# One pool of eight PSUM banks, and more work for the DMA transposes, in a fused attention and channel-mix kernel

## The chip, the cores and the metric

The kernel runs on one core of a Trainium2 chip. The metric is the device time of one execution in microseconds, as the median of several runs. A profile is one execution recorded instruction by instruction; its span, from the first to the last instruction, is a little shorter than its device time.

## What is computed

Sliding-window attention with a linear position bias (batch 8, 8 heads, 576 positions, head size 64, window 128) feeds a channel mix of width 512 with an inner width of 1024. Inputs and output are float32; the kernel computes in bfloat16 and accumulates in float32.

```python
scores = scale * q @ k.T                      # per batch and head, 576 x 576
mask   = (rel >= 0) & (rel < 128)             # rel = query position - key position
scores = where(mask, scores - slope[h] * |rel|, -1e9)
x      = softmax(scores) @ v                  # heads side by side: (8, 576, 512)

x_prev = x shifted by one position
xk = mu_k * x + (1 - mu_k) * x_prev
xr = mu_r * x + (1 - mu_r) * x_prev
k  = relu(xk @ w_k)                           # 512 -> 1024
out = sigmoid(xr @ w_r) * (k * k @ w_v)       # 1024 -> 512
```

## The kernel before

**Attention.** A batch has four head pairs g. For each, q and k are brought into a transposed layout `qk` or `qx` (64 head elements of two heads on 128 partitions). `scores` (its matmuls are L726, in batch 0 with a bias product, L713) multiplies keys by queries with 64 rows, both heads at once on the two halves of the array, only inside the window; the keys' 4.5 blocks of 128 are done in two halves, HALF0 and HALF1, each with up to 512 columns for each of two heads, which is two banks of PSUM. ScalarE takes the exponential (L740) into `at`, VectorE multiplies by a mask (L753) that holds window and bias, and `attend` (L781) multiplies by v with a column of ones, so that the denominators come out beside the sums; VectorE takes reciprocals (L787) and writes the normalized `xu` (L793).

**Transposes.** The output `xu` has positions on the partitions, the channel mix wants channels there (`xt`). Three ways are in use, chosen by batch: `out_t` by full transposes on TensorE (L820, batch 0), `out_some` by half transposes on TensorE in two row tiles for two head pairs at a time (L837, batches in `OH`) with a ScalarE copy out of PSUM (L696), and `out_flip` by a DMA transpose on SP's queue (batches in `XO`; the crossbar). The same holds for q and k: TensorE (`qk_quad`, `qk_some`: L1078, L837) up to batch 3, DMA transposes (`flip`, `qx<-cb`) from batch 4 on. The last 64 positions of q and k, the tails, go through `tails_full` (four transposes on TensorE, L912, and a VectorE copy) or through `tail_flip` (a DMA transpose `tt<-ts`, batches in `XTT`). A change between matmuls that use 64 rows of the array and those that use 128 is called a row change here.

**Channel mix.** `shift` forms x minus its predecessor (`dl`, L880) and the two mixtures `xk`, `xr` (L887) on VectorE. `channel_mix` then runs over pieces of 256 to 512 positions: eight groups of four matmuls with `wk_sb` (L983), a relu on ScalarE (L990), a square on VectorE or ScalarE (L964, L962); per 128 positions four matmuls with `wr_sb` (L1001), a tanh on ScalarE (L1008), eight with `wv_sb` (L1017) and VectorE's product of both (L1022), which SP's queue stores (L1047).

**Order.** Every step is a node of a plan. `ORDER` gives TensorE, ScalarE and VectorE a fixed sequence of nodes, written out in the file; the plan walks through it with assumed durations and hands out buffers (`Hold`, by class) as they come free, and in doing so sets the order of SP's and POOL's queues. Engines then wait for each other by semaphores. 90 small matmuls on a zero tile (`warm`, L687) are nodes like others and stand where the order puts them. Loads are issued by POOL with a cast to bfloat16.

**PSUM.** Two tiles of two banks (`duo`, class `p2`) serve scores and attention; four of one bank (`uno`, class `p1`) serve all the rest. Both halves of a head pair's scores are one node, which takes both `duo` at once:

```python
_, (m0, m1) = scores(b, g, [HALF0 + (None,), HALF1 + (htt,)], ...)
```

`n_split` halves some of the late stores, so that the number of hardware DMAs is a multiple of eight.

## Time and profile before

| | |
|---|---|
| median of 3 runs | 229.41 us (228.8 to 229.55) |
| profiled execution | 228.84 us |
| its span | 227.1 us |
| TensorE (PE) busy | 221.8 us, 98% |
| VectorE (DVE) busy | 188.8 us, 83% |
| ScalarE (ACT) busy | 155.0 us, 68% |
| mean granted TensorE clock | 0.998 |

Lines of the profile name the engine (PE matmuls, PEld weight loads, DVE, ACT, POOL, SP), the source line, the operation, what it writes and reads, the count, the busy time, the mean duration in ns, and the idle time of the engine before it with what ended it. In a table by stage, each engine has its busy time and its count of instructions. The chain of waits runs from the last instruction back through whatever released each step; its rows show a start, a length and the work.

### The profile page before, as it was taken

The page shows a single profiled execution, that of the slowest core. Times are in us where ns is not written, and L with a number is a line of the kernel's source. Part 1 is how long each engine was busy: PE and PEld are TensorE (multiplying, and loading weights), DVE is VectorE, ACT ScalarE, POOL GpSimd, SP SyncE. Part 2 cuts the span into 40 slices and gives each one's busy share as a digit, 9 for nine tenths or more (in the row PEclk, how much of TensorE's full clock was granted, in tenths as well). Part 3 has the DMA queues.
Part 4 walks back from the last instruction along what each step waited for, and adds up shares of the span by engine and source line. Part 5 has one row for each costly group of instructions (what it writes and reads, how often), then busy time and mean ns, then how long its engine had stood idle before and what let it go on. Part 6 is the DMA issues. An engine that isn't in the chain of part 4 may idle for free.

```text
span 227.1 us, 6442 instructions
## 1 busy us (share of the span) xinstructions
PE 221.8 (98%) x2587; PEld 133.2 (59%) x2587; DVE 188.8 (83%) x423; ACT 155.0 (68%) x279; POOL 92.0 (41%) x118
## 2 busy tenths in 40 slices
PE   8899999999999999999999999999999999999994
PEld 8576766755666755556666554546765455446552
DVE  6786999899879998899978996999899988963433
ACT  0678999999989984975868358768567564047511
POOL 8856726599962964385208750240000000000000
PEclk9999999999999999999999999999999999999999
DMA  6999999999999999999999999999150415430124
GB/s 165 179 185 200 197 196 175 199 180 151 196 156 165 137 130 180 168 182 147 211 180 158 120 185 231 177 136 222 30 135 3 123 46 52 131 136 3 49 92 139
DMA packets 129981, 33.19 MB, mean 146 GB/s; under 512 B 116632, under 2 KB 126112, under 8 KB 129952
## 3 DMA queue, kind: packets, MB, share of 16 engines
q0 software_dynamic: 95728, 16.26, 97.5%
q1 hardware_dynamic: 32480, 15.94, 34.1%
q10 hardware_dynamic: 1744, 0.59, 1.1%
q8 instruction: 20, 0.33, 0.6%
q14 instruction: 9, 0.07, 0.1%
HBM read 33.56 MB, written 9.44 MB: 189 GB/s over the span
## 4 chain that ended last, share of the span: by engine, by line
PE 92%; ACT 3%; DMA 2%; SPq 1%; issue 0%; DVE 0%; DVEq 0%; ACTq 0%
PE uno L983 28%; PE uno L1017 28%; PE uno L1001 13%; PE duo L726 7%; PE duo L781 7%; DMA qx<-in_q_dram 2%; PE uno L837 2%; PE uno L1078 2%; ACT at L740 1%; PE duo L713 1%; ACT qk L696 1%; PE uno L781 1%; SPq L550 1%; PE uno L687 1%; PE uno L820 1%; PE uno L939 0%
## 5 line engine op out<-in xcount | busy, mean ns | idle before, releaser
L983 PE MATMUL uno<-xk,wk_sb 128*128 128x256 bf16 (+2 forms) x416 | 72.0, 314 | 0.1
L740 ACT ACTIVATE at<-duo 128x1024 bf16<-128x1024 f32 (+2 forms) x68 | 65.5, 985 | 8.8 <-PE duo L726 8.5
L1017 PE MATMUL uno<-wv_sb,kk 128*128 128x512 bf16 (+2 forms) x296 | 69.7, 374 | 0.0
L990 ACT ACTIVATE rl<-uno 128x256 bf16<-128x256 f32 (+2 forms) x104 | 46.4, 471 | 26.4 <-PE uno L983 21.0
L983 PEld LDWEIGHTS <-wk_sb 128*128 128x128 bf16 x416 | 38.7, 98 | 24.2 <-issue 0.3
L1017 PEld LDWEIGHTS <-kk 128*128 128x128 bf16 x296 | 27.2, 98 | 27.3
L500 POOL DMA_DIRECT2D vs<-in_v_dram x32 | 28.4, 904 | 31.8 <-PE duo L781 25.9
L753 DVE TENSOR_TENSOR at<-at,mask 128x1024 bf16<-128x1024 bf16 x56 | 36.9, 682 | 1.8 <-ACT at L740 1.8
L964 DVE TENSOR_TENSOR kk<-rl 128x256 bf16<-128x256 bf16 (+2 forms) x94 | 30.2, 339 | 8.8 <-ACT rl L990 8.4
L1008 ACT ACTIVATE rs<-uno 128x512 bf16<-128x512 f32 x36 | 21.1, 604 | 22.2 <-PE uno L1001 22.1
L1001 PE MATMUL uno<-wr_sb,xr 128*128 128x512 bf16 x144 | 36.1, 379 | 0.0
L1022 DVE SCALAR_TENSOR_TENSOR ot<-rs,uno 128x512 f32<-128x512 bf16 (+2 forms) x37 | 24.4, 666 | 10.5 <-PE uno L1017 8.8
L887 DVE SCALAR_TENSOR_TENSOR xk<-dl,mu_sb,xt 128x576 bf16<-128x576 bf16 (+1 forms) x32 | 24.4, 779 | 0.0
L887 DVE SCALAR_TENSOR_TENSOR xr<-dl,mu_sb,xt 128x576 bf16<-128x576 bf16 (+1 forms) x32 | 24.3, 776 | 0.0
L781 PEld LDWEIGHTS <-at 128*128 128x128 bf16 x576 | 21.0, 97 | 4.7 <-ACT at L740 0.4
L793 DVE TENSOR_TENSOR xu<-duo,rc 128x640 bf16<-128x640 f32 x28 | 22.6, 815 | 0.2
L1001 PEld LDWEIGHTS <-xr 128*128 128x128 bf16 x144 | 13.3, 98 | 13.5 <-issue 0.2
L531 POOL DMA_DIRECT2D cb<-in_k_dram x20 | 17.5, 888 | 6.9 <-DMA vs<-in_v_dram 4.7
L781 PE MATMUL duo<-vs,at 128*128 128x65 bf16 x448 | 18.6, 193 | 0.0
L531 POOL DMA_DIRECT2D cb<-in_q_dram x20 | 17.7, 935 | 1.2 <-PE duo L781 1.1
L696 ACT COPY xt<-uno 128x640 bf16<-128x640 bf16 (+3 forms) x28 | 15.0, 583 | 3.3 <-PE uno L837 2.5
L880 DVE TENSOR_TENSOR dl<-xt 128x576 bf16<-128x576 bf16 (+1 forms) x32 | 13.5, 432 | 2.8 <-ACT xt L696 2.7
(83 smaller groups left out, 197.9 us busy)
## 6 DMA issues: line engine op xcount, KB each, us to landing
out_dram<-ot SPq DMA_DIRECT2D x30, 256.0 KB, 4.6
vs<-in_v_dram POOLq DMA_DIRECT2D x32, 128.0 KB, 7.8
cb<-in_q_dram POOLq DMA_DIRECT2D x20, 128.0 KB, 6.3
cb<-in_k_dram POOLq DMA_DIRECT2D x20, 128.0 KB, 12.1
out_dram<-ot SPq DMA_DIRECT2D x10, 128.0 KB, 1.8
wk_sb<-in_moe_w_k_dram POOLq DMA_DIRECT2D x2, 512.0 KB, 9.1
cb<-in_q_dram POOLq DMA_DIRECT2D x4, 256.0 KB, 9.7
cb<-in_k_dram POOLq DMA_DIRECT2D x4, 256.0 KB, 8.6
```

The lines of the kernel that those rows point to most:

```text
L500: return dma(POOL, 256, issue_t(1024), lambda e: nc.gpsimd.dma_start(out=vs_buf[h.idx][:, j, :, 0:D], in_=v[b, :, 128 * j:128 * j + 128].r ...
L531: return [dma(POOL, 256, issue_t(1024), lambda e, r=r: nc.gpsimd.dma_start(out=cb_buf[h.idx][:, i, r], in_=src[:, :, r]), [g], kind="q") f ...
L740: lambda e, ah=ah, w=w, hp=hp: nc.scalar.activation(out=ah(), in_=two(hp)[:, :, 0:w], func=AF.Exp, scale=float(scale)), (), [hp])
L753: nc.vector.tensor_tensor(out=a, in0=a, in1=m, op=ALU.mult)
L781: nc.tensor.matmul(a[:, hl, t - t0], lhsT=at[:, lo:lo + 128], rhs=vs[:, u, 2 * g + hl, 0:W] if u < NF else tvb[:, 2 * g + hl, 0:W], start= ...
L887: lambda e: nc.vector.scalar_tensor_tensor(out=buf[hk.idx][:, g, e0 + c0:e0 + c1], in0=dls(), scalar=mu[:, g:g + 1], in1=xc(1), op0=ALU.mu ...
L964: nc.vector.tensor_tensor(out=out, in0=in_, in1=in_, op=ALU.mult)
L983: nc.tensor.matmul(one(hp)[:, 0:n], lhsT=wk_sb[:, po, 128 * fo:128 * fo + 128], rhs=xk_buf[hx.idx][:, po, c0:c1], start=(po == 0), stop=(p ...
L990: a = op(ACT, act_t(n), [s], pr, lambda e, hp=hp, hr=hr: nc.scalar.activation(out=rl_buf[hr.idx][:, 0:n], in_=one(hp)[:, 0:n], func=AF.Rel ...
L1001: nc.tensor.matmul(one(hp), lhsT=xr_buf[hx.idx][:, po, 128 * c:128 * c + 128], rhs=wr_sb[:, po], start=(po == 0), stop=(po == NPO - 1))
L1017: nc.tensor.matmul(one(hv)[:, a:b], lhsT=kk_buf[hk.idx][:, fo, o:o + 128], rhs=wv_sb[:, fo, a:b], start=(fo == 0), stop=(fo == NFO - 1))
L1022: nc.vector.scalar_tensor_tensor(out=ot_buf[ho.idx][:, a:b], in0=rs_buf[hs.idx][:, a:b], scalar=1.0, in1=one(hv)[:, a:b], op0=ALU.add, op1 ...
```

## The change

PSUM becomes four tiles of two banks, and its eight banks are one class `p`. A step takes one bank or an aligned pair; single banks are taken first from pairs that are already broken. As the framework orders accesses by tile, `use` declares for each one-bank access that it does not depend on the accesses of other engines to the tile's other bank; dependences through a second shared tile are kept. Each score half is a node of its own with its own pair (`SS`). The output of batch 5 goes through DMA transposes (`XO` from 5, `OH` up to 4), and so do the tails of batch 3 (`XTT` from 3). `ORDER` is a new sequence for all three engines. With these numbers `n_split` goes from 5 to 0. Two paths that were not in use, a mask through TensorE and full transposes of q and k, are deleted.

```diff
-    XO = range(6, B)
+    XO = range(5, B)
-    SS = ()
-    OH = range(1, 6)
+    SS = range(1, B)
+    OH = range(1, 5)
-    XTT = range(4, B)
-    MMASK = False
+    XTT = range(3, B)
...
-    duo = [pst.tile([128, 2, 512], FP32, name=f"duo{i}") for i in range(2)]
-    uno = [pst.tile([128, 512], FP32, name=f"uno{i}") for i in range(4)]
+    duo = [pst.tile([128, 2, 512], FP32, name=f"duo{i}") for i in range(4)]

     def one(h):
-        return uno[h.idx if h.cls == "p1" else N1 + h.idx]
+        return duo[h.idx // 2][:, h.idx % 2]

     def two(h):
-        return duo[h.idx]
+        return duo[h.idx // 2]
+
+    def use(h, x, other=None):
+        if h.n == 1:
+            here = x.ins.engine
+            both = shared.setdefault((other.cls, other.idx), []) if other else []
+            for e in (ENG.PE, ENG.Activation, ENG.DVE):
+                if e != here:
+                    tc.declare_no_dep(x.ins, group=f"{e}{h.idx ^ 1}", keep=both,
+                                      reason="the tile's other bank")
+            tc.add_to_no_dep_group(f"{here}{h.idx}", x.ins)
+            if other:
+                both.append(x.ins)
+        return x
...
-    plan = Plan(dict(qx=2, p2=2, p1=N1, pt=4 - N1, qk=NQ, ...), {}, WAIT)
+    plan = Plan(dict(qx=2, p=8, qk=NQ, ...), {"p": (0, 2, 4, 6)}, WAIT)
...
-            todo.append((pieces, m0, tt, a0, w, Hold("p2")))
+            todo.append((pieces, m0, tt, a0, w, Hold("p", 2)))
...
-        hp, hx = Hold("p1" if 2 * nt * W <= 512 else "p2"), Hold("xu")
+        hp, hx = Hold("p", 1 if 2 * nt * W <= 512 else 2), Hold("xu")
...
-                nc.tensor.transpose(
-                    tp()[:, 128 * t:128 * t + 128],
-                    xu_buf[hx.idx][:, t].rearrange("p h d -> p (h d)"), ident)
+                transpose(
+                    hp, tp()[:, 128 * t:128 * t + 128],
+                    xu_buf[hx.idx][:, t].rearrange("p h d -> p (h d)"), ident, other=hx)
...
```

The branch that `SS` switches on was in the file already:

```python
if b in SS:
    s0, (m0,) = scores(b, g, [HALF0 + (None,)], False, hq, ha, ..., [ha], [hq])
    _, (m1,) = scores(b, g, [HALF1 + (htt,)], False, hq, ha, ... + [(s0, 0.0)], prio, [], [hq, htt])
```

## The prediction

> **What bounds the kernel now.** I read the page first (engine shares, slices), then the windows by stage, then the chain of waits, then groups of instructions and DMA issues. The profiled execution took 228.84 us, 227.1 of them the span and 1.7 around it; the three runs have a median of 229.41 (228.8 to 229.55), 0.6 above the profiled one. The sum below is made against 228.84.

> ```profile
> span 227.1 us, 6442 instructions
> PE 221.8 (98%) x2587; PEld 133.2 (59%) x2587; DVE 188.8 (83%) x423; ACT 155.0 (68%) x279; POOL 92.0 (41%) x118
> PE 92%; ACT 3%; DMA 2%; SPq 1%; issue 0%; DVE 0%; DVEq 0%; ACTq 0%
> ```

> TensorE is busy for 98% and makes 92% of the chain that ended last. By stage (the cuts are the first real group at 5.03 us, the first weight product at 17.36 and the last matmul's end at 223.82):

> ```profile
> core 0: us, PE busy (x) PEld busy (x) DVE busy (x) ACT busy (x) POOL busy (x), PEclk, DMA share, GB/s
> 0.00:5.03 5.03, 4.04 (x47) 4.04 (x47) 3.54 (x19) 0.00 (x0) 4.04 (x11) 1.00 0.59 156
> 5.03:17.36 12.33, 11.51 (x175) 7.74 (x173) 9.33 (x38) 8.55 (x18) 8.79 (x13) 1.00 1.75 185
> 17.36:50.00 32.64, 32.48 (x649) 22.15 (x650) 29.18 (x69) 31.01 (x66) 20.86 (x27) 1.00 1.69 192
> 50.00:190.00 140.00, 140.00 (x1537) 81.28 (x1536) 126.34 (x255) 103.17 (x171) 58.31 (x70) 1.00 1.52 147
> 190.00:223.82 33.82, 33.82 (x189) 17.96 (x186) 20.01 (x44) 12.27 (x26) 0.00 (x0) 1.00 0.27 84
> 223.82:227.10 3.28, 0.00 (x0) 0.00 (x0) 0.40 (x2) 0.00 (x0) 0.00 (x0) 0.83 0.37 131
> ```

> From 17.36 to 223.82 us TensorE is idle for 0.16 us in all. What lies outside is 5.03 us of start, 0.82 of idle up to 17.36, and a tail of 3.28. Busy alone could hide short stalls, so I look at the rate in one piece of the chain of waits (start, us, what):

> ```profile
> 89.17 1.73 PE uno L1001 x8
> 90.90 0.40 PE uno L837 x20
> 91.30 0.44 PE duo L726 x12
> 91.74 0.97 PE uno L1017 x4
> 92.71 3.48 PE uno L983 x16
> 96.19 0.55 PE duo L726 x12
> 96.73 0.29 PE uno L837 x20
> 97.03 2.70 PE uno L1017 x12
> ```

> Sixteen 512-column matmuls take 3.48 us, 0.87 for four. After a block of 64-row work (scores L726, half transposes L837) the first four take 0.97, and scores take 0.55 after 128-row work but 0.44 after 64-row work; L837 likewise 0.40 and 0.29. So a change of row mode costs 0.10 to 0.11 us, and nothing else in this piece is lost. The kernel is bound by TensorE's work plus its row changes, almost without waits. Any bank that comes free earlier has 0.16 us to give after 17.36.

> **The change part by part.**

> ```profile
> L837 PE MATMUL uno<-ident,xu 64*128 64x64 bf16 x200 | 4.6, 190 | 0.0
> L912 PE MATMUL uno<-ident,ts 128*128 128x128 bf16 x12 | 1.2, 219 | 0.0
> L696 ACT COPY xt<-uno 128x640 bf16<-128x640 bf16 (+3 forms) x28 | 15.0, 583 | 3.3 <-PE uno L837 2.5 <-PE uno L820 0.8
> L696 DVE COPY tt<-uno 128x512 bf16<-128x512 bf16 x3 | 1.3, 422 | 0.5 <-PE uno L912 0.5
> ```

> *Output of batch 5 by the crossbar* (XO from 5, OH to 4). Two blocks of 20 half transposes leave TensorE. The group row gives 4.6/10 = 0.46 us a block with its row change and drain; the chain's 0.29 is the block between 64-row neighbours. I take 0.29 here and count row changes apart: 2 x 0.29 = 0.58 us, all on the path. ScalarE loses four copies (4 x 0.583 = 2.3 us), which were beside matmuls: nothing.

> *Tails of batch 3* (XTT from 3). Four transposes leave: 1.2/3 = 0.4 us by the row, which holds the last one's latency; 4 x 0.055 = 0.22 is the stream alone. I take 0.3. VectorE's copy of 0.42 us goes too, off the path.

> *Score halves alone* (SS). Each half of the scores of batches 1 to 7 takes its own pair of banks, where before one step took both pairs. Matmuls and exponentials are the same in number; only the neighbours move. The cost is the row changes. In the built order before there are 100 changes between 128-row and 64-row matmuls, after it 94 (26 and 26 up to the last bias matmul, 74 and 68 behind it). That is 6 x 0.105 = 0.63 us less; most of it belongs to the two blocks that went. Had each of the 28 second halves come to stand by itself between 128-row work, 56 changes more would cost 56 x 0.105 = 5.9 us and the sum would be +5.0 (233.8) instead of -1.5; since the built order lays halves of different head pairs side by side and the count falls, that gets no chance. [...]

> *One pool of eight banks, no waits between a tile's banks.* It removes a wait that hardly exists: 0.16 us of idle after 17.36. I set it at 0, with a bound of -0.2. A mask through TensorE and full-width transposes that go out of the file were not in use: 0.

> *Start.* The 90 warm-up matmuls stay 90:

> ```profile
> L687 PE MATMUL uno<-warm 128*128 128x128 bf16 x90 | 8.8, 250 | 1.0 <-DVE warm L469 1.0
> 0.99 4.26 PE L687 MATMUL uno<-warm 128*128 128x128 bf16 x47 [0.99 <-DVE warm L469]
> 5.31 0.72 PE L687 MATMUL uno<-warm 128*128 128x128 bf16 x10
> 7.99 1.06 PE L1123 MATMUL uno<-id,qx 128*128 128x128 f32 x7 [0.48 <-DMA qx<-in_q_dram]
> ```

> After, 54 stand ahead of the first real group (47 before), but 60 ahead of the first bias matmul (61 before). Seven more at (0.72 - 0.22)/9 = 0.056 us put the first group 0.39 us later and the first scores at the same place. The other 30 stand between part-0 and part-1 work up to the 449th matmul (217th before). They are in the order whether TensorE has work or not, so the time lost to them is the same. The wait of 0.48 us for the float32 q goes neither way. The third score group of part 0 no longer waits for the first exponential to free a pair of banks, and its heads' exponentials still queue on ScalarE. I set the start at 0, and bound it: -0.8 if all 0.82 us of idle before 17.36 goes, +1.5 if ScalarE's queue (31.01 busy of 32.64 us behind it, so about to become the limit) is met by three exponentials in a new order.

> *Five DMA transposes more* (four xt, one tt), on SP's queue:

> ```profile
> qx<-cb SPq DMA_TRANSPOSE x32, 7.5
> xt<-xu SPq DMA_TRANSPOSE x8, 2.6
> tt<-ts SPq DMA_TRANSPOSE x4, 7.1
> L793 DVE TENSOR_TENSOR xu<-duo,rc 128x640 bf16<-128x640 f32 x28 | 22.6, 815 | 0.2
> L887 DVE SCALAR_TENSOR_TENSOR xk<-dl,mu_sb,xt 128x576 bf16<-128x576 bf16 (+1 forms) x32 | 24.4, 779 | 0.0
> L753 DVE TENSOR_TENSOR at<-at,mask 128x1024 bf16<-128x1024 bf16 x56 | 36.9, 682 | 1.8 <-ACT at L740 1.8
> L1022 DVE SCALAR_TENSOR_TENSOR ot<-rs,uno 128x512 f32<-128x512 bf16 (+2 forms) x37 | 24.4, 666 | 10.5 <-PE uno L1017 8.8
> L964 DVE TENSOR_TENSOR kk<-rl 128x256 bf16<-128x256 bf16 (+2 forms) x94 | 30.2, 339 | 8.8 <-ACT rl L990 8.4
> L787 DVE RECIPROCAL rc<-duo 128x10 f32<-128x10 f32 x28 | 6.1, 217 | 4.3 <-PE duo L781 3.3 <-ACT qk L696 0.5
> ```

> The xt ones of batches 6 and 7 landed in 2.6 us with the loads over; batch 5's fall among loads, as the qx ones did, so I take 7.5. Who waits is VectorE at dl, with everything queued behind it (masks, squares, evictions). In the built order there are 19 VectorE instructions between the first head pair's xu and its dl: three each of xu 0.815, shift products 0.78, masks 0.68, evictions 0.67 and reciprocals 0.22, and four squares 0.34, together 10.9 us. That covers 7.5 with 3.4 to spare; the last pair has 23 instructions of the same kinds in between. On SP the transposes of batch 6's tail and of batch 7's q and k, and the stores, stand behind them and behind the wait for xu, later by 4 x 1.2 us of issue; before, batch 7's last one went out like this, ahead of its first scores:

> ```profile
> 153.45 1.23 SPq L535 DMA_TRANSPOSE qx<-cb  x1
> 167.85 0.56 PE L726 MATMUL duo<-qx 64*128 64x256 bf16 x8
> ```

> Of these 14.4 us a landing takes 7.5 and the delay at most 4.8. Batch 3's tail, in 7.1 us, has its loads and the first halves' scores ahead of its use. Cost 0, up to +1 if a landing takes over 11 us.

> *Stores.* The number of hardware DMAs becomes a multiple of eight, so none of the late stores is halved (ten of 128 KB become five whole). They lie 3 to 7 row blocks ahead of the last one; the two stores that end the kernel stay. 0.

> Sum: -0.58 - 0.3 - 0.63 = -1.5 us, so 228.84 - 1.5 = 227.3 against the profiled run and 227.9 against the median. I take 227.4. Bounds of the terms: -0.92 - 0.4 - 0.63 - 0.2 (banks) = -2.2 at best; -0.58 - 0.22 = -0.8 if the row changes bring nothing; upward, the start's +1.5 and the landing's +1.

> **The rivals.**

> *A new wait for ScalarE in the dense start (slower).* Place: 17 to 50 us. ScalarE leaves 1.63 us idle of 32.64 there, VectorE 3.46, and the order of all three engines is new.

> ```profile
> L740 ACT ACTIVATE at<-duo 128x1024 bf16<-128x1024 f32 (+2 forms) x68 | 65.5, 985 | 8.8 <-PE duo L726 8.5
> ```

> If halves that run ahead fill the banks until an exponential of 0.985 us frees one, TensorE, which has no slack, waits for it. It decides from the point where more than about 1.5 such waits come; three make +3.0, so 228.84 - 1.5 + 3.0 = 230.3. For it: those idle shares, and that SS lets scores run ahead. Against: eight banks in one pool, and ScalarE's load falls by no more than 2.3 us but elsewhere.

> *What leaves TensorE comes back as a wait (no change), 228.8.* From 50 to 190 us VectorE is busy for 90% and ScalarE for 74%; a bound by VectorE would need 10% more. The chance of 0.10 holds 0.03 for TensorE not being the limit at all: weight loads (PEld) are busy for 59%, and if the other 41% were room, the removed 1.5 us would change nothing. The chain's piece speaks against: 16 matmuls in 3.48 us follow each other at 0.217 us, without room. [...]

> *A start that shrinks too:* -1.5 - 0.8 gives 226.5. Against it stand the 90 warm-ups in the order.

> That the pool does nothing by itself is part of the forecast.

> **How the numbers follow.** Forecast (226.6 to 228.4: 228.84 less 2.2, and less 0.8 with 0.4 for the runs' spread): 0.60. Shorter start (around 226.5): 0.09. No change: 0.10. New wait (229.6 to 231.5): 0.21. About 0.3% (0.7 us) is what a measurement of this kernel can tell from no change. Of the forecast's 0.60, 0.03 falls within it. Faster 0.57 + 0.09 = 0.66, same 0.03 + 0.10 = 0.13, slower 0.21. The range 226.2 to 229.8 leaves out some 0.04 below and 0.14 above; the forecast's own is 226.6 to 228.4.

> **What would show it.** Right: 2543 matmuls, PE busy near 220.3 us and still 98%; no half transposes with the xu of batch 5; under 0.5 us of TensorE idle from the first weight product on; four-matmul groups at 0.87 and 0.97 as before; twelve xt transposes, the new ones landing in 7 to 8 us, and no VectorE idle time put down to them. Wrong: idle time of weight loads or matmuls put down to ACT at the exponential between 17 and 50 us, dl waiting for a DMA, or SP's transposes of batch 7 landing behind the work that asks for them.

## The result, and the profile after

The changed kernel takes 229.99 us (median of 18 runs, 229.06 to 232.28), the kernel before 229.37 on the same chip (18 runs, 228.8 to 229.7). The ratio is 1.0047, with a 95% interval of 1.003 to 1.0064: slower by half a per cent, where 227.4 was forecast. It also scatters: 3.2 us between its fastest and slowest execution, 0.9 in the kernel before. The profiled execution is the fastest one, 229.06, of which the span is 227.3. Four executions of the runs below took over 1.5% longer than the fastest of the same kernel, and the times given are medians without them.

The page of the changed kernel, its engine line, the chain and two rows of the DMA queues (packets, MB, share of 16 engines):

```profile
span 227.3 us, 6340 instructions
PE 220.3 (97%) x2543; PEld 131.2 (58%) x2543; DVE 188.2 (83%) x426; ACT 151.1 (66%) x271; POOL 92.0 (40%) x118
...
q0 software_dynamic: 95728, 16.26, 99.7%
...
q8 instruction: 20, 0.33, 0.6%
...
PE 92%; DMA 2%; issue 1%; DVE 1%; ACT 1%; SPq 1%; DVEq 0%
```

TensorE's work fell from 221.8 to 220.3 us, the forecast 1.5. The span did not follow. Its stages, with the cuts of the prediction:

```profile
core 0: us, PE busy (x) PEld busy (x) DVE busy (x) ACT busy (x) POOL busy (x), PEclk, DMA share, GB/s
5.03:17.36 12.33, 11.26 (x194) 7.40 (x191) 8.83 (x40) 7.07 (x13) 8.61 (x12) 1.00 1.75 185
17.36:50.00 32.64, 31.18 (x641) 21.50 (x641) 28.73 (x71) 30.48 (x66) 21.27 (x28) 1.00 1.70 193
50.00:190.00 140.00, 139.81 (x1455) 79.78 (x1456) 125.86 (x254) 101.88 (x168) 58.11 (x70) 1.00 1.61 154
...
223.82:227.30 3.48, 0.15 (x3) 0.00 (x0) 0.57 (x2) 0.00 (x0) 0.00 (x0) 1.00 0.37 129
```

TensorE's idle time by stage: 1.07 us up to 17.36 (0.82 before), 1.46 from there to 50 (0.16 before), 0.19 to 190 (0.00 before), 3.33 at the end (3.28 before). That is 0.25 + 1.30 + 0.19 + 0.05 = 1.8 us more, against 1.5 us less work. So 1.3 us of the loss lies in the dense start. The waits of TensorE in that stage are one row (engine, line, tile, releaser: us in total, times, longest):

```profile
PE duo L397 <- issue: 1.4, 2, 0.8
```

No engine and no DMA is named: "issue" is time in which TensorE waited for nothing that the profile shows. L397 is the helper through which transposes go, as L394 is that of most other matmuls; scores are L748 (L756 where an edit adds lines above them). The timeline of TensorE shows both places:

```profile
28.64 0.38 PE L397 MATMUL duo<-ident,cb 64*64 64x64 bf16 x22
29.57 0.55 PE L397 MATMUL duo<-ident,cb 64*64 64x64 bf16 x42 [0.56 <-issue]
...
48.30 0.29 PE L397 MATMUL duo<-ident,xu 64*128 64x64 bf16 x7
49.40 0.38 PE L397 MATMUL duo<-ident,xu 64*128 64x64 bf16 x13 [0.81 <-issue]
```

Both stalls fall inside a block of equal small transposes, behind the 22nd of 64 and the 7th of 20. Nothing changes there: same line, same source, same tile, no wait. What does lie there shows when the instructions are counted, here TensorE's matmuls and weight loads up to the first stall and between the two:

```profile
0.00:29.30 29.30, 26.95 (x478) 20.07 (x478) 21.22 (x85) 19.71 (x43) 20.64 (x32) 1.00 1.41 185
29.30:49.20 19.90, 18.92 (x384) 12.47 (x384) 18.67 (x42) 18.78 (x37) 12.49 (x16) 1.00 1.83 191
```

384 + 384 = 768 = 3 x 256. And the instruction queue moved 20 packets and 0.33 MB, which is 16 KB a packet; with 5086 matmuls and weight loads in the kernel, or 254 a packet, a packet of 256 instructions fits, which would be 64 bytes each. This gave the theory.

**Theory B**: a wait on data of batches 1 and 2 that the profile doesn't attribute. **Theory C**: the difference is spread over the span. Another one, D, comes with the last pair of runs.

### The profile page after: what moved, and what is told of

It is laid out like the page before. It is cut to its first block, busy times and chain, and to the rows that moved or that the text cites. A ratio compares the mean times of both kernels' runs of the same rounds, so it can differ in the third digit from the quotient of the medians.

```text
span 227.3 us, 6340 instructions
## 1 busy us (share of the span) xinstructions
PE 220.3 (97%) x2543; PEld 131.2 (58%) x2543; DVE 188.2 (83%) x426; ACT 151.1 (66%) x271; POOL 92.0 (40%) x118
## 4 chain that ended last, share of the span: by engine, by line
PE 92%; DMA 2%; issue 1%; DVE 1%; ACT 1%; SPq 1%; DVEq 0%
PE duo L394 79%; PE duo L748 8%; PE duo L397 4%; DMA qx<-in_q_dram 2%; PE duo L735 1%; SPq L569 1%; ACT at L762 0%; DVE qk L715 0%; ACT rl L1012 0%; DVE ot L1044 0%; DVE tv L499 0%; ACT xt L715 0%; DVE rc L809 0%; DVE xu L815 0%; ACT qk L715 0%
## 5 line engine op out<-in xcount | busy, mean ns | idle before, releaser
L394 PE MATMUL duo<-xk,wk_sb 128*128 128x256 bf16 (+2 forms) x416 | 70.6, 314 | 0.0
L394 PE MATMUL duo<-wv_sb,kk 128*128 128x512 bf16 (+2 forms) x296 | 69.3, 374 | 0.0
L1012 ACT ACTIVATE rl<-duo 128x256 bf16<-128x256 f32 (+2 forms) x104 | 45.5, 476 | 28.4 <-PE duo L394 21.3
L394 PEld LDWEIGHTS <-wk_sb 128*128 128x128 bf16 x416 | 38.6, 98 | 22.0 <-issue 1.0
L394 PEld LDWEIGHTS <-kk 128*128 128x128 bf16 x296 | 27.0, 98 | 29.3 <-issue 1.8
L1030 ACT ACTIVATE rs<-duo 128x512 bf16<-128x512 f32 x36 | 21.1, 610 | 27.8 <-PE duo L394 27.7
L394 PE MATMUL duo<-wr_sb,xr 128*128 128x512 bf16 x144 | 36.0, 379 | 0.2 <-ACT rl L1012 0.2
L1044 DVE SCALAR_TENSOR_TENSOR ot<-rs,duo 128x512 f32<-128x512 bf16 (+2 forms) x37 | 24.3, 668 | 6.8 <-PE duo L394 4.7
L815 DVE TENSOR_TENSOR xu<-duo,rc 128x640 bf16<-128x640 f32 (+2 forms) x36 | 26.7, 744 | 0.3
L394 PEld LDWEIGHTS <-at 128*128 128x128 bf16 x576 | 21.8, 97 | 5.9 <-ACT at L762 0.6
L909 DVE SCALAR_TENSOR_TENSOR xr<-dl,mu_sb,xt 128x576 bf16<-128x576 bf16 (+1 forms) x32 | 24.7, 780 | 0.1
L909 DVE SCALAR_TENSOR_TENSOR xk<-dl,mu_sb,xt 128x576 bf16<-128x576 bf16 (+1 forms) x32 | 24.4, 779 | 0.1
L394 PE MATMUL duo<-vs,at 128*128 128x65 bf16 x512 | 22.3, 193 | 0.3 <-ACT at L762 0.2
L394 PEld LDWEIGHTS <-xr 128*128 128x128 bf16 x144 | 13.4, 98 | 13.8 <-issue 0.4
L809 DVE RECIPROCAL rc<-duo 128x10 f32<-128x10 f32 (+2 forms) x36 | 7.6, 211 | 10.3 <-PE duo L394 7.5
L715 ACT COPY qk<-duo 128x512 bf16<-128x512 bf16 (+1 forms) x24 | 13.5, 602 | 2.1 <-PE duo L397 2.1
```

Of the source, the lines that this page charges most:

```text
L394: return use(h, nc.tensor.matmul(*a, **k))
L815: use(hp, nc.vector.tensor_tensor(out=out_, in0=a5()[:, :, :, 0:D], in1=rc[:, :, 0:nt, None].to_broadcast([128, 2, nt, D]), op=ALU.mult), hx)
L909: lambda e: nc.vector.scalar_tensor_tensor(out=buf[hk.idx][:, g, e0 + c0:e0 + c1], in0=dls(), scalar=mu[:, g:g + 1], in1=xc(1), op0=ALU.mu ...
L1012: a = op(ACT, act_t(n), [s], pr, lambda e, hp=hp, hr=hr: use(hp, nc.scalar.activation(out=rl_buf[hr.idx][:, 0:n], in_=one(hp)[:, 0:n], fun ...
L1030: lambda e, hp=hp, hs=hs: use(hp, nc.scalar.activation(out=rs_buf[hs.idx], in_=one(hp), func=AF.Tanh, scale=0.5), hs), [hs], [hp])
L1044: use(hv, nc.vector.scalar_tensor_tensor(out=ot_buf[ho.idx][:, a:b], in0=rs_buf[hs.idx][:, a:b], scalar=1.0, in1=one(hv)[:, a:b], op0=ALU. ...
```

## The experiments

### The changed kernel once more, and its page borders moved

No edit in the first run; it is a second profiled execution.

> The changed kernel unaltered, for a second profiled execution. Theory A (instruction fetch): TensorE gets its instructions in pages of 256 (16 KB, the instruction queue of the profile moves 20 of them); the next page is asked for when one is entered and is there 4.2 to 5.9 us later; a page that runs through in less stalls at its end. The pages entered at about 24.8, 39.9 and 43.9 us need 4.1, 4.1 and 3.9 us of work. So a slower execution than the profiled 229.06 has its time in longer stalls at the same two places (about 28.6 us, inside the transposes of batch 1, and 48.5 us, inside the half transposes of batch 1) or a third one at about 44.5 us, each 0.5 to 2 us with no releaser, and PE busy stays 220.3. Theory B (a wait on data that the profile does not attribute, a load of batch 1 or 2): stalls at the same places, but the time differs by waits put to DMA or ACT. Theory C: the difference between executions is spread over the whole span.

It took 229.91 us. Its waits without a releaser in transposes (us in total, times, longest) and its TensorE timeline at the second place:

```profile
PE duo L397 <- issue: 2.0, 2, 1.7
...
48.29 0.29 PE L397 MATMUL duo<-ident,xu 64*128 64x64 bf16 x7
50.25 0.37 PE L397 MATMUL duo<-ident,xu 64*128 64x64 bf16 x13 [1.67 <-issue]
```

The same transposes, but 1.67 us instead of 0.81. That is 0.86 us, and the execution is 0.85 us slower than the first profiled one. Laid side by side, the weight loads of the two traces differ by at most 0.24 us up to this place, and by 0.85 to 0.86 us from there to the end. (The first stall is 0.36 us in this execution.) So a usual execution of 230.0 is the profiled 229.06 with a longer stall, as far as this one shows, and C falls.

The next edits move the page borders through the work at little cost in time (with 16 instructions more, the block of the first stall begins at 28.84 us, 28.64 without): some of the warm-up matmuls at the very start, which all stand ahead of the first real group, are made as two halves, or two are made as one.

```
     def emit_warm(e):
+        if halved[0]:                     # 8 in the first run
+            halved[0] -= 1
+            for c in (0, 64):
+                matmul(h_wm, one(h_wm)[0:64, c:c + 64], lhsT=warm[:, 0:64], rhs=warm[:, 0:64], ...)
+            return
```

> The changed kernel with eight of its first warm-up matmuls each made as two of half the size: 16 instructions more ahead of everything else, the same time for them, all else as it was. Theory A (instruction fetch in pages of 256): the page borders fall 8 matmuls earlier in the work, so the first stall moves from behind the 22nd to behind the 14th of the second pair's transposes of batch 1 and the second one from behind the 7th half transpose to just ahead of the block; the pages need 4.7, 5.1 and 3.8 us instead of 4.1, 4.1 and 3.9, so with 4.85 us from page to page the stalls sum to 1.2 us instead of 2.5: faster than the changed kernel by about 1.2 us (228.6 to 229.0). Theory B (a wait on data): the stalls stay behind the same matmuls, the time stays at 229.9 to 230.0.

```
     def emit_warm(e):
+        if merged[0]:                     # 32 in this run
+            merged[0] -= 1
+            if merged[0] % 2 == 0:
+                matmul(h_wm, one(h_wm)[:, 0:256], lhsT=warm,
+                       rhs=warm[:, None, :].to_broadcast([128, 2, 128]), ...)
+            return
```

> The changed kernel with 32 of its first warm-up matmuls made as 16 of double width: 32 instructions fewer ahead of everything else, the same time for them, all else as it was. Theory A (instruction fetch): page borders fall 16 matmuls later in the work; the pages there need 3.5, 3.9 and 3.9 us instead of 4.1, 4.1 and 3.9, so at 4.85 us from page to page the stalls sum to 3.4 us instead of 2.5: slower than the changed kernel by about 0.9 us (230.5 to 231.2), and the first stall shows 16 matmuls later. Theory B (a wait on data): no change, 229.9 to 230.0, stalls behind the same matmuls as before.

With 32 instructions fewer: 231.74 us (1.012 of the kernel before, 1.0079 to 1.0161), 1.8 us slower than the changed kernel's 229.99, without any work added. TensorE's timeline at its three stalls:

```profile
31.29 0.41 PE L397 MATMUL duo<-ident,cb 64*64 64x64 bf16 x26 [1.64 <-issue]
...
47.88 0.40 PE L397 MATMUL duo<-ident,xu 64*128 64x64 bf16 x15 [1.38 <-issue]
...
52.43 0.28 PE L756 MATMUL duo<-qk 64*128 64x256 bf16 x1 [0.81 <-issue]
```

The counts up to the first stall and between the stalls, by windows of the same kernel:

```profile
0.00:30.50 30.50, 27.97 (x478) 20.09 (x478) 22.15 (x87) 20.41 (x45) 20.98 (x33) 1.00 1.41 186
30.50:47.00 16.50, 15.11 (x254) 9.83 (x256) 14.76 (x34) 14.57 (x28) 9.67 (x13) 1.00 1.84 189
47.00:52.00 5.00, 3.69 (x127) 2.61 (x128) 3.40 (x8) 3.95 (x10) 5.00 (x7) 1.00 2.23 171
```

Between the stalls lie 256 + 256 and 128 + 128 instructions (three matmul records are missing). The first stall again stands behind 478 matmuls, though 16 fewer lie ahead: in the work it has moved from 42 transposes before the end of their block to 26, that is 16 later. The third stall stands among scores, not transposes. B expected the stalls to stay at their matmuls and the time to stay; it falls. The size was forecast too small (230.5 to 231.2): these pages took 4.6 to 5.5 us from entry to entry, not 4.85. Not all of the difference is stalls: of the 3.1 us by which this profiled span (230.4) is longer than the changed kernel's, they make 2.5 (3.83 against 1.37), and a wait for a load of the tails (`ts`) at 16 us another 0.4.

With 16 instructions more: 231.99 us (1.0101, 1.0067 to 1.0134), where A with 4.85 us a page gave 228.6 to 229.0. The place was right, the size and even the sign wrong. Its profiled execution has only one stall, again at a border, now ahead of the half transposes:

```profile
47.02 0.81 PE L394 MATMUL duo<-wv_sb,kk 128*128 128x512 bf16 x2
...
50.40 0.39 PE L394 MATMUL duo<-wv_sb,kk 128*128 128x512 bf16 x1 [2.57 <-issue]
...
51.34 3.38 PE L394 MATMUL duo<-wv_sb,kk 128*128 128x512 bf16 x8
```

Here the packet started 4.1 us after the page was entered (1.7 to 3.7 in the first 50 us of the changed kernel), and TensorE stood for 2.57 us. Then something followed that no theory had: eight 512-column matmuls took 3.38 us, where eight take 1.9 elsewhere. The windows ahead of and behind the end of the stall give the granted clock (the column after POOL):

```profile
46.50:50.70 4.20, 1.58 (x23) 0.72 (x11) 4.20 (x7) 2.50 (x6) 4.20 (x6) 1.00 2.41 156
50.70:55.00 4.30, 4.30 (x37) 1.91 (x36) 0.03 (x1) 2.60 (x4) 4.30 (x6) 0.60 2.42 157
```

The 0.60 is a mean over the window: by the trace the clock was 0.50 from 51.6 to 55.0 us. So this stall cost twice: 2.57 us of wait, and 1.5 us more in the eight matmuls behind it, at a clock of 0.50. Of this kernel's six executions five took 231.6 to 232.2, with a granted clock of 0.990 to 0.993, and one 229.52, with 1.0. The changed kernel's own scatter fits: its four executions of 231.95 to 232.28 are those with a granted clock of 0.991 to 0.993. Behind the 1.67 us of the second profiled execution the clock did not drop: its granted clock is 1.0.

### The kernel before, made to stall

The same edit in the kernel before, with 36 warm-up matmuls halved.

> The kernel before with 36 of its first warm-up matmuls each made as two of half the size: 72 instructions more, the same time for them. Theory A (instruction fetch): the shortest page of the kernel before, now 4.84 us of work entered at 44.8 us, becomes one of 3.99 us entered at 43.8 us, so at 4.85 us a page a stall of 0.85 us appears near 47.8 us with no releaser: 0.85 us slower than before (229.8 to 230.4 where the kernel before gives 229.4). Theory B: no change.

It took 230.23 us (1.0032, 1.0015 to 1.005), 0.8 slower than the kernel before and within its range; a stall appeared where it was expected, in a block of 32 transposes that runs through otherwise:

```profile
48.18 0.44 PE L1086 MATMUL uno<-ident,cb 64*64 64x64 bf16 x30
49.19 0.22 PE L1086 MATMUL uno<-ident,cb 64*64 64x64 bf16 x2 [0.57 <-issue]
```

The stall thus belongs neither to the pool of banks nor to the new order as such: the kernel before has it too, as soon as its borders fall badly.

### The fetch by itself

```
             def emit2(e, f0, f1, a, b, hv, o=o, i=i):
+                if f0 == 0 and i == 0 and a == 0 and order in (2, 8, 14):
+                    for k in range(512):
+                        hl = k % 2
+                        nc.tensor.transpose(one(hv).bitcast(BF16)[64 * hl:64 * hl + 64, 0:64],
+                                            warm[0:64, 0:64], ident[0:64, 0:64])
```

> The kernel before with three bursts of 512 small transposes (64 by 64, 1024 instructions, four pages each) put ahead of a wv group: of batch 0/1 (about 60 to 80 us, loads in full swing), of batches 4/5 (about 160 to 190 us) and of batches 6/7 (after the loads). It measures the disputed cost by itself; the bursts only add work. Theory A (instruction fetch): within a page the transposes follow each other in 13 to 27 ns, so 128 of them need 1.7 to 3.4 us; at each page border TensorE stands still until 4.2 to 6.8 us after the last border while the software DMA queue is busy, with no releaser, and the borders lie 256 instructions apart; where the loads are over the interval is shorter, about 3 us or less (1.6 us to ask, 0.9 for the packet, some for the hand-over), so the last burst is the fastest. Theory B (the small transposes themselves are slowed by something else, evenly): equal steps without stalls at 256 instructions, or stalls at other distances. The whole kernel becomes 30 to 60 us longer by A.

280.51 us, 51 more. TensorE's timeline in the first burst (loads at full when it begins) and the third (after the loads):

```profile
66.66 2.46 PE L1019 MATMUL uno<-ident,warm 64*64 64x64 bf16 x143
72.01 10.43 PE L1019 MATMUL uno<-ident,warm 64*64 64x64 bf16 x369 [2.89 <-issue]
...
249.70 4.24 PE L1019 MATMUL uno<-ident,warm 64*64 64x64 bf16 x256
254.87 2.96 PE L1019 MATMUL uno<-ident,warm 64*64 64x64 bf16 x128 [0.94 <-issue]
258.33 3.62 PE L1019 MATMUL uno<-ident,warm 64*64 64x64 bf16 x128 [0.49 <-issue]
```

The windows around the two bursts, with the share of the DMA engines in the last column but one:

```profile
60.00:70.00 10.00, 9.12 (x283) 7.00 (x281) 6.34 (x16) 8.16 (x16) 6.27 (x8) 1.00 2.31 153
250.00:262.00 12.00, 10.52 (x506) 10.27 (x499) 0.00 (x0) 0.40 (x1) 0.00 (x0) 0.74 0.02 5
```

The instruction queue of this run moved 32 packets and 0.52 MB, 12 packets more than in the kernel before, for 2 x 1536 = 3072 more matmuls and weight loads: 256 a packet. All five stalls lie at borders, 128 transposes and their 128 weight loads apart in the last burst. With the DMA engines at 2.31 the page entered at 66.9 us had its packet 2.8 us later and its successor 5.1 us later; at 0.02 the packet started 1.0 us after entry and the pages followed each other in 3.2 and 3.5 us. Not every border stalled: from 72 to 83 us the clock was at 0.50 and the DMA engines nearly idle (0.02), so that a page of slowed transposes took 3.7 us by itself, longer than these 3.2 and 3.5 us.

### The same steps in other orders

These runs were to keep the work and lengthen the pages. The first two moved many steps between 12 and 80 us.

> The changed kernel with the same steps in another order between about 12 and 80 us (some 70 of 418 steps of TensorE, 85 of VectorE and 39 of ScalarE stand elsewhere in their lists: pairs of transposes of batches 1 and 2 with weight groups between them, attend steps apart) and 30 of the first warm-up matmuls made as two halves each (60 instructions, same time). Matmuls, DMAs and pools are those of the changed kernel. No page of 256 TensorE instructions holds under 5.2 us of work then (4.1, 4.1 and 3.9 us before the reordering). Theory A (instruction fetch): at 4.85 us a page the stalls of 2.5 us in a usual run go; the steps stand a little less well otherwise (0 to 1.5 us more waiting), so 227.5 to 229.0, faster than the kernel before, with PE busy still 220.3 us and no idle without a releaser over 0.3 us between 17 and 60 us. Theory B (the order of the changed kernel waits for data or ScalarE in the dense start): the stalls stay in the same places, 229.5 to 231.

> Another such reordering of the changed kernel, without extra instructions: no page under 5.2 us of work, but shorter ones near it than in the first reordering (sum of what is missing to 6.2 us a page: 2.4 us instead of 1.4; the changed kernel 6.5). Theory A: 227.7 to 229.5, between the first reordering and the kernel before, some executions with a stall of 0.5 to 1 us at a page border. Theory B: 229.5 to 231.

230.34 us (1.0045, 1.0029 to 1.0061) and 231.36 (1.0101, 1.0082 to 1.0121): no gain, and both ranges missed. One border still stalled in the first, by 0.5 us, 0.8 less than the two in the profile of the changed kernel; but its span is 0.7 us longer, so some 1.5 us came in elsewhere. All of that lies ahead of 105 us: from there to the end its weight loads start 0.7 to 0.8 us behind the changed kernel's. (TensorE's idle time can't be read from this trace after that: matmul records are missing, 813 beside 824 weight loads from 105 to 190 us.) A new order costs as much as the stalls, so these runs decide nothing. Smaller moves, in TensorE's list alone (the numbers are steps of `ORDER`; behind `/` the new sequence):

```
 mv2: -286 294 312 333 / +333 286 294 312
      -366 498 510 306 314 381 468 319 315 463 513 320 516 317
      +317 366 498 510 306 314 381 468 319 315 463 513 320 516
 mv4: -269 93 224 275 / +93 224 275 269;   -381 468 319 / +319 381 468
      -288 286 294 312 333 375 345 / +286 294 345 312 288 333 375
 mv5: mv2 with 381 468 turned into 468 381, and
      -322 122 257 239 324 369 209 278 339 342 283 / +209 322 122 257 239 283 324 369 278 339 342
```

> The changed kernel with two of TensorE's steps moved and nothing else touched: the attend step of batch 1, first head pair, three places ahead, and one wr group (four 512-column matmuls) 13 places ahead, to between the transposes of batch 2 and the attend steps. The pages entered at about 38 and 44 us then hold 5.6 and 4.8 us of work instead of 4.1 and 3.9; the one at 24.8 us keeps 4.1. Theory A (instruction fetch): at 4.85 us a page the stalls fall from 2.5 to 0.8 us, so 228.3 to 229.0 unless the wr group comes before its input (then some of it is spent waiting for VectorE); the idle at 28.6 us stays, the one at 48.5 us goes or halves. Theory B (a wait on data of batches 1 and 2): the stall at 48.5 us stays in the same half transposes, 229.9 to 230.2.

> The changed kernel with four of TensorE's steps moved by 2 to 4 places and nothing else touched (the attend step of batch 1, second head pair, three ahead; a wv group of batch 0 two ahead; a wk group four back; a wk group three back). The pages entered at about 24.7, 38.9 and 43.9 us then hold 4.2, 5.0 and 4.7 us of work instead of 4.1, 4.1 and 3.9. Theory A: stalls of 0.8 us instead of 2.5 at 4.85 us a page, so 228.3 to 229.2. Theory B: no change, 229.9 to 230.2.

> The changed kernel with five of TensorE's steps moved and nothing else touched: the two of the run with two moves, one of the two wr groups of batch 0's first part five places ahead to between the transposes of batch 1, an output transpose of batch 0 six places ahead, an output transpose of batch 1 one place back. The pages entered at about 24.8, 38.3 and 43.9 us then hold 5.1, 5.6 and 5.0 us of work instead of 4.1, 4.1 and 3.9. Theory A: no stall at 4.85 us a page (2.5 before), 0.3 at 5.2: 227.5 to 228.5, faster than the kernel before, unless moved steps now wait for their inputs (those waits would carry a releaser). Theory B: no change, 229.9 to 230.2.

Four short moves: 229.17 us where the kernel before took 228.95 (1.0009, 0.9996 to 1.0022), so 0.9 us better against it than the changed kernel, at the upper end of its range, and all twelve executions within 228.8 to 230.1. Its profiled execution is one of the slowest (229.96) and still has 1.4 us of stalls. The two others took 231.98 (1.0129, 1.0103 to 1.0156) and 232.12 (1.0128, 1.0112 to 1.0144), far above their ranges. By their waits, the long moves put steps ahead of what they need; the waits of TensorE with two moves:

```profile
PE duo L397 <- issue: 1.9, 2, 1.5
...
PE duo L748 <- ACT at L762: 0.9, 1, 0.9
...
PE duo L394 <- ACT at L762: 0.8, 2, 0.6
...
PE duo L748 <- ACT xt L715: 0.8, 1, 0.8
```

2.5 us of waits for ScalarE, the kind of wait that the prediction's first rival had in mind, and stalls of 1.9 us beside them, since the page entered at 45.1 us took 6.2 us here. The clock fell too, to 0.50 from 52.3 to 55.7 us: behind a stall of 1.50 us and, 0.4 us later, the last of these waits. Two last attempts:

> The changed kernel with the steps between about 13 and 60 us in another order (some 80 of TensorE's 418 steps, 80 of VectorE's and 70 of ScalarE's stand elsewhere) and 29 of the first warm-up matmuls made as two halves each; matmuls, DMAs and pools as in the changed kernel. The order was sought for long pages and few waits: the shortest pages hold 5.1 us of work (entered at 23 us) and 5.8 us (at 42.5 us), where the changed kernel has 4.1, 4.1 and 3.9. Theory A (instruction fetch): no stall without a releaser of over 0.3 us, none of the executions near 232 us, 228.0 to 229.3; of the 2.5 us of stalls of a usual run 1 to 1.5 us may come back as waits with a releaser, since the order is otherwise less worked out. Theory B: stalls without a releaser stay, 229.9 or more.

> The run with four of TensorE's steps moved, with two of the first warm-up matmuls made as two halves each (four instructions, same time). Theory A: the page entered at 24.5 us holds 4.4 instead of 4.2 us of work, those at 38.9 and 43.8 us stay at 5.0 and 4.7, so 0.2 us less of stall: 0 to 0.3 us faster than the run with four moves, level with the kernel before or up to 0.3 us faster. Theory B: no change against the run with four moves.

229.82 (1.003, 1.0018 to 1.0041) and 229.42 (1.0008, 0.9994 to 1.0023). The first lies above its range, with one stall of 0.5 us left and a wait of 0.9 us for an exponential. The page that ends in that stall held 5.8 us of work, but its packet started only 4.3 us after entry. The second is level with the kernel before and with the run with four moves, which both theories allow. No order that was tried beats the kernel before, so whether the forecast gain exists was still open.

### Is the stall all that is lost?

Theory D: what left TensorE comes back as waits whatever the fetch does. In this pair both kernels load only two of the eight heads in the later batches, so that by A the next page comes about as fast from about 42 us on as in the last burst (3.2 and 3.5 us); the right results of the other heads are left out thereby.

```
+    def HL(b, b0):
+        return 2 if b >= b0 else H
...
-            out=vs_buf[h.idx][:, j, :, 0:D],
+            out=vs_buf[h.idx][:, j, 0:HL(b, 2), 0:D],          # v and its tails from batch 2
...
-            out=cb_buf[h.idx][:, i, r], in_=src[:, :, r]), ...
+            out=cb_buf[h.idx][:, i, r, 0:HL(b, 3)], in_=src[:, 0:HL(b, 3), r]), ...   # q, k, tails from batch 3
```

> The kernel before with the loads of q, k and tails from batch 3 on and of v from batch 2 on cut to two of the eight heads (the rest of these buffers keeps what older batches left; weights, stores and all work on the engines stay). It is the partner of the next run, for the same cut in both. Both theories: PE busy as in the kernel before (221.8), span within 1 us of it, since its TensorE hardly waits; 228.3 to 229.6.

> The changed kernel with the same cut of the loads. Theory A (instruction fetch, slow only while the software DMA queue is busy): from about 42 us on that queue has a quarter of its bytes, so the next page comes in 3.2 to 4 us as after the loads in the run with bursts; the stalls at 44.5 and 48.5 us go (0.8 to 2 us in the changed kernel), that at 28.6 us (0.5 us, loads of batches 1 and 2, uncut) stays. Then the 1.5 us of TensorE work that left must show: faster than its partner by 0.4 to 1.0 us, where the uncut pair stands 0.6 to 1.1 us the other way. Theory D (what left TensorE comes back as waits for other engines or worse order, whatever the fetch): slower than its partner, as in the uncut pair.

With lighter loads the kernel before takes 229.30 us, its old time (0.9998, 0.9987 to 1.0009). The changed kernel takes 228.14 (0.9947, 0.9933 to 0.996, of the unaltered kernel before; five executions, 227.8 to 228.3): 1.2 us ahead of its partner, where the uncut one is 0.6 behind. TensorE's timeline of the changed kernel with light loads:

```profile
28.58 0.37 PE L397 MATMUL duo<-ident,cb 64*64 64x64 bf16 x22
29.32 0.55 PE L397 MATMUL duo<-ident,cb 64*64 64x64 bf16 x42 [0.36 <-issue]
...
48.04 0.47 PE L397 MATMUL duo<-ident,xu 64*128 64x64 bf16 x20
```

The stall at 28.6 us is there, with the loads of batches 1 and 2 uncut. The twenty half transposes at 48 us now run through; the page that ends in them took 3.9 us, and its packet started 0.75 us after entry instead of 2.7. Against the trace of the changed kernel the weight loads gain 0.2 us at the first border and 1.0 us at this one, and otherwise keep step to 0.1 us from 8 us on. The 1.5 us of removed work less the 0.36 us still lost make 1.1 us, where the pair differs by 1.2, a little over the forecast 0.4 to 1.0. D falls: nothing in the work of TensorE, VectorE and ScalarE changed between the two pairs, and the sign did.

All traces together say the same. Fourteen of them hold 26 stalls of TensorE of over 0.3 us without a releaser. Counted from the start in matmuls, weight loads and semaphore instructions, every one stands at 193 or 194 modulo 256, and in every one TensorE goes on 1.2 to 1.6 us after the end of the packet that started while the page in front was running, be the stall 0.34 or 3.32 us long.

## Why the prediction was wrong

**What bounds the kernel: right.** TensorE makes 92% of the chain in both.

**The terms of the sum: right.** 2543 matmuls and 220.3 us of TensorE work were named and measured, -1.5. This checks their sum, not each term. Half transposes with xu fell from 200 to 160. Row changes cost what they did; four wv or wk matmuls behind 64-row work in the chain of the changed kernel, with scores beside them:

```profile
91.24 0.32 PE duo L748 x4
91.57 0.97 PE duo L394 x4
92.53 0.32 PE duo L748 x4
92.86 0.29 PE duo L397 x20
```

**Transposes by DMA at no cost: right.** The DMA issues of the changed kernel (the last number is the median, in us, from issue to landing):

```profile
xt<-xu SPq DMA_TRANSPOSE x12, 4.4
...
tt<-ts SPq DMA_TRANSPOSE x5, 8.5
```

and VectorE's wait at dl (us in total, times, longest):

```profile
DVE dl L902 <- ACT xt L715: 1.1, 3, 0.5
```

Four of the twelve, issued between 128 and 146 us, landed in a median of 8.3 us, a little over the 7.5 taken, and no wait of VectorE is put down to them.

**Start at 0: nearly right.** 0.25 us more of idle time, within the bounds of -0.8 and +1.5. It is one execution of each: the wait for q at the start takes up to 0.9 us in the traces of these kernels and is missing in some.

**The step that failed** is the one on the score halves: "Matmuls and exponentials are the same in number; only the neighbours move. The cost is the row changes." Neighbours had a second price here. Which small matmuls shared a page had a part in whether TensorE got its instructions in time (it stood for 0.56 and 0.81 us at two borders), and no term of the sum stood for that. The count of instructions was in the profile (2587 pairs), and so was the instruction queue with its 20 packets; neither was read. The missing term measures 1.37 us in the profiled execution (0.56 + 0.81) and 2.03 in the second one (0.36 + 1.67), with 1.5 more in the run whose clock fell to 0.50. With 2.0 the forecast -1.5 becomes +0.5; +0.6 was measured.

**The rivals.** "A new wait for ScalarE in the dense start" had the place (17 to 50 us) and nearly the time (230.3 against 230.0), but by luck, for the mechanism is another: TensorE's waits in that stage name no engine, and ScalarE's only show up in the reordered runs, where steps were moved ahead of their inputs. Of the signs of being right two failed: TensorE was idle for 1.65 us from the first weight product to 190 us, where under 0.5 was named, and busy for 97%, not 98%. None of the three signs that were to show the prediction wrong appeared; the sign that did, "issue" inside a block of equal instructions, was not on the list. "TensorE not the limit" falls too: the light pair gives the removed work back as time.

## What to carry to other kernels

Where a TensorE-bound order is changed, count instructions as well as microseconds: cut TensorE's list into pages of 256 matmuls and weight loads and look for pages with little work in them, above all blocks of small transposes while loads run. How little is too little varies: here one page of 4.2 us ran through, and one of 5.8 us did not. A stall marked "issue" in the middle of equal instructions is the sign, and a count between two such stalls that is a multiple of 256 pointed to the fetch here (768, and 512 and 256 with 32 instructions fewer). Move an instruction or two at the front before trusting a difference of half a per cent between two orders: moving the borders alone was worth 0.8 to 2.0 us here.

## What was not expected of the hardware

- Where TensorE had to wait, it took 3.2 to 3.5 us from entering one page to running the next with idle DMA engines (share of 0.02) and 4.6 to 6.6 us with busy ones (shares of 0.9 to 2.6 over the page), and it differs between executions of one kernel: 0.81 and 1.67 us of stall at the same transpose.
- In the dense part of the changed kernel a packet starts 1.7 to 3.7 us behind the first instruction of a page. Among the 512-column matmuls after 165 us it starts 0.9 to 3.0 us ahead of it (195.1 against 198.1 us), so there it was not asked for by the entry; what asked for it was not shown.
- A stall of 2.57 us was followed by 3.4 us at 0.50 of the clock (51.6 to 55.0 us, with 16 instructions more), and so was one of 1.50 us with a wait of 0.76 us close behind it (52.3 to 55.7 us, with two moves); one of 1.67 us alone was not (the changed kernel once more). In the last burst, of nothing but 64x64 transposes, the clock fell behind a stall of 0.94 us (to a mean of 0.74 from 250 to 262 us).
- The instruction fetch moves 0.33 MB in all, 0.6% of the DMA engines' time, and still TensorE stood 1.37 us at its borders in the profiled execution: the share of this queue did not show who waits for it.
